# Six instead of four first-product blocks made in halves, with a new order and bank plan, in a linear-attention and FFN kernel

## The chip, the cores and the metric

One core of one Trainium2 chip runs the whole kernel. The metric is the device time of one execution in microseconds (us), lower is better. Engines: TensorE (PE matmuls, PEld weight loads), VectorE (DVE), ScalarE (ACT), GpSimd (POOL) and SyncE (SP), which issues most DMAs here.

## The reference, cut to what matters

```python
def _A_ref(x, wqkv, wo):                      # x: (1, 2048, 512), 32 heads of 16
    qkv = (x @ wqkv).reshape(B, S, 3, H, Dh).transpose(2, 0, 3, 1, 4)
    q, k, v = qkv[0], qkv[1], qkv[2]
    phi = lambda t: jnp.where(t > 0, t + 1, jnp.exp(t)) + 1e-6
    pq, pk = phi(q), phi(k)
    kv = jnp.einsum("bhsd,bhse->bhde", pk, v)
    z = jnp.einsum("bhsd->bhd", pk)
    num = jnp.einsum("bhqd,bhde->bhqe", pq, kv)
    den = jnp.einsum("bhqd,bhd->bhq", pq, z)[..., None] + 1e-6
    return (num / den).transpose(0, 2, 1, 3).reshape(B, S, D) @ wo
def _B_ref(x, w1, w2):                        # w1: (512, 1792), w2: (1792, 512)
    return jnp.maximum(x @ w1, 0) @ w2
h = x + _A_ref(_layernorm(x), wqkv, wo)
out = h + _B_ref(_layernorm(h), w1, w2)
```

All tensors are bf16.

## The kernel before, in words

The 2048 tokens are 16 tiles of 128, in four chunks of 512 (chunk c holds tiles 4c to 4c+3). Nothing is scheduled by a compiler: the string ORDER (L18 to L54) is a list of words, each of them calls one small function with the numbers behind its dots (L563 to L566), and each engine runs its instructions in the order in which the words issued them. Semaphores follow from the data. The last or next to last number of a word on TensorE is mostly the PSUM bank (0 to 7; a bank holds 128 x 512 f32), so the string is also the bank plan. A bank can be written anew only when its last reader has finished.

The words that matter, in the order of a tile's way:

- `lx`, `lk`, `lq`, `lv`, `lo`, `l1`, `l2`: loads of x and of the weights, issued on SP (L220, L226).
- `S.t`, `A.t` (VectorE, L254, L255): statistics and their aggregate of tile t; `R` (ScalarE, L260, L261): 1/sqrt; `N.t` (VectorE, L268): the first layernorm. `T.t.b` (TensorE, L293) and `E.t` (ScalarE, L303) transpose tiles 0 to 4 into lnT; `X.t` (SP, L314) does it by a DMA transpose for the others.
- `K.t.b` (L322) and `Q.c.j.b` (L330): the products for k (of a tile) and q (of a chunk, 128 of the 512 columns). `F`, `U` (ScalarE, L340, L343), `M`, `D` (VectorE, L347, L350) make phi of k out of them, `qF`, `qU`, `qM`, `qD` phi of q (pqT).
- `G.t` (L374) sums over the tokens into banks 4 to 7, `z` (L398), `kv` (L420), `m.j.b` (L432) form what all queries share: the matrix of k and v times wo (m_sb), copied out by `mD` (VectorE) and `mA` (ScalarE).
- `d4.c.b` (TensorE, L446; `d4.2.b.2` does chunks 2 and 3 into two banks), `dl4.c`, `dx4.c` (ScalarE, L452, L457): the reciprocal of the denominator of chunk c. `wb.c` (SP, L474) writes it to DRAM, eight `rb.c.h` (SP, L477; for chunk 0 also `ab` on ScalarE's queue) read it back spread over the partitions, and two `dm.c` (VectorE, L493) multiply pqT by it.
- `h.t.b` (TensorE, L502) gives the attention output of tile t, `hD.t` (VectorE, L508) adds x. `s.t`, `a.t`, `n.t` (VectorE, L256, L257, L276; `nA.t` for tiles 0 and 1 on ScalarE, L282) make the second layernorm without its scale, `x.t` (SP, L315) transposes it by DMA into lnT.
- `p.c.f.b` (L517): block f (of 14) of the FFN's first product for chunk c, four matmuls of 512 tokens. `ph.c.f.b.half` (L526): the same block for 256 of the 512 tokens (half 0: tiles 4c and 4c+1, half 1: 4c+2 and 4c+3), four matmuls of half the width into one half of the bank. `pD.c.f.2` (VectorE, L537) or `pA.c.f.2` (ScalarE, L532) empties two banks, f and f+1, with the relu.
- `f.t.b.f0.n` (L546): the second product of tile t, n of the 14 parts; `fo.t` (VectorE, L554) scales by `r` and adds h, `fd.t` (SP, L561) stores it.

Before the change, after the last Q block TensorE makes four first-half blocks of chunk 0 (f = 2, 3, 0, 1), and then turns to the second halves and whole blocks, which need tiles 2 and 3. The blocks ahead of the first of these hide what tiles 2 and 3 still have to go through: hD, s, a, n and the transposes x.3 and x.2.

Of the kernel before, what the change touches and what calls it, by code (L numbers as in the profile page):

```python
# [16 lines left out]

ORDER = """  # L18
table const lx.0.1 warm.66.7.64 lx.1.1 masks lx.2.1 lk.0.4 lx.3.1 S.0 lx.4.2 S.1 lx.6.2 lq.0.4 A.0 A.1 S.2 R.0.1
warm.2.7 lx.8.4 R.1.1 N.0 lx.12.4 A.2 N.1 T.0.1 R.2.1 T.1.5 E.0 N.2 E.1 T.2.2 S.3 K.0.0 E.2 A.3 S.4 K.2.2.2.2  # L20
R.3.1 K.2.2.0.2 F.0.1 N.3 S.5 U.0.1 T.3.3 K.1.6.0.2 E.3 A.4 A.5 K.1.6.2.2 S.7 R.4.2 K.3.1.0.2 M.0.1 F.1.1 S.6
K.3.1.2.2 U.1.1 Q.0.1.5 N.4 F.2.1 A.6 N.5 A.7 F.3.1 T.4.6 M.1.1 X.5 D.0.1 Q.0.0.4 R.6.2 D.1.1 M.2.1 U.3.1 M.3.1
Q.0.2.0 N.7 lo.0.2 E.4 S.9 X.7 U.2.1 Q.0.3.1 N.6 qU.0.0.2 D.3.1 K.4.2 S.15 X.6 qF.0.0.2 S.8 K.5.3 D.2.1 qM.0.0.2
qF.0.2.2 G.3 A.8 A.9 S.12 R.8.2 G.0 S.14 F.4.2 N.9 G.2 A.12 N.8 X.9 U.4.2 S.13 G.1 A.15 A.14 A.13 qD.0.0.2 X.8
R.12.2 K.6.2 qU.0.2.2 M.4.2 S.11 K.7.3 lv.0.2 R.14.2 N.12 N.13 X.12 K.9.1 S.10 F.6.2 D.4.2 K.8.0 U.6.2 lv.2.2 A.10
M.6.2 X.13 G.4 N.14 U.8.2 N.15 D.6.2 G.5 X.15 F.8.2 za.4.1 G.6 A.11 X.14 M.8.2 K.12.0 R.10.2 qM.0.2.2 N.10 K.13.1
N.11 X.10 D.8.2 G.7 za.6.0 F.12.2 X.11 K.14.2 U.12.2 qD.0.2.2 K.15.3 M.12.2 l1.2.2 za.8.0 l2.0.7 K.10.0 F.14.2
D.12.2 K.11.1 U.14.2 zf G.9 M.14.2 F.10.2 D.14.2 G.8 U.10.2 zhi M.10.2 G.12 zlo D.10.2 G.14 z.1.0 z.2.0 z.3.0
z.0.0 G.15 zc zh d4.0.3 G.11 dl4.0 dx4.0 G.10 wb.0 G.13 lo.2.2 Q.1.0.1 gA.2.2 gD.0.2 rb.0.6 Q.1.1.2 ab.0.3 rb.0.2
ab.0.7 rb.0.4 kv.0.0 kv.2.0 ab.0.1 rb.0.0 kv.1.0 kv.3.0 ab.0.5 l1.0.2 Q.1.3.6 kx qF.1.0.2 Q.1.2.5 qU.1.0.2  # L30
qM.1.0.2 m.0.3 m.1.4 Q.2.3.7 qF.1.2.2 mD.0.2 Q.2.1.1 qU.1.2.2 qM.1.2.2 dm.0.0.2 m.2.3 m.3.4 Q.2.0.0 dm.0.2.2
mA.2.2 qD.1.0.2 h.1.6 qU.2.0.2 qD.1.2.2 h.0.2 hD.1 qF.2.0.2 h.3.3 s.1 hD.0 Q.2.2.6 a.1 s.0 nA.1 d4.1.2 a.0 h.2.1
hD.3 x.1 nA.0 s.3 qF.2.2.2 Q.3.0.5 x.0 a.3 hD.2 dl4.1 Q.3.3.4 n.3 qU.2.2.2 s.2 x.3 Q.3.2.3 a.2 dx4.1 n.2 Q.3.1.6
qM.2.0.2 qF.3.2.2 x.2 qM.2.2.2 ph.0.2.0.0 qU.3.2.2 qM.3.2.2 ph.0.3.1.0 wb.1 ph.0.0.2.0 qF.3.0.2 qD.3.2.2
ph.0.1.3.0 qD.2.2.2 ph.0.1.3.1 qU.3.0.2 ph.0.0.2.1 qM.3.0.2 rb.1.6 p.0.11.7 rb.1.3 pD.0.0.2 rb.1.1 ph.0.3.1.1
rb.1.0 p.0.10.6 qD.2.0.2 rb.1.7 qD.3.0.2 rb.1.4 p.0.9.2 rb.1.2 pD.0.10.2 rb.1.5 p.0.6.5 l2.7.7 d4.2.6.2 ph.0.2.0.1
dl4.2 p.0.5.4 r.0.4 dm.1.0.2 dl4.3 p.0.4.3 dx4.2 dm.1.2.2 h.4.7 pD.0.2.2 wb.2 pA.0.4.2 p.0.7.6 dx4.3 hD.4 p.0.8.1
pD.0.6.2 h.5.7 pD.0.8.2 rb.2.4 p.0.13.4 rb.2.7 rb.2.3 hD.5 h.6.5 rb.2.0 rb.2.6 f.1.2.0.7 hD.6 rb.2.5 s.5 rb.2.2
rb.2.1 p.0.12.3 wb.3 h.7.1 pD.0.12.2 f.0.7.7.7 hD.7 s.4 f.2.4.0.7 s.7 a.5 a.4 dm.2.0.2 f.1.2.7.7 n.4 dm.2.2.2 a.7
n.5 rb.3.2 s.6 rb.3.6 h.9.0 rb.3.3 h.8.1 x.4 hD.9 a.6 f.0.7.0.7 n.7 r.4.4 fo.1 x.7 n.6 s.9 f.3.5.0.7 rb.3.1 x.6  # L40
h.10.0 x.5 h.11.3 f.3.5.7.7 f.2.4.7.7 fo.3 hD.8 fd.3 rb.3.7 p.1.13.2 fo.2 rb.3.4 fd.1 hD.11 p.1.12.1 rb.3.5 a.9
fo.0 fd.2 p.1.2.6 rb.3.0 hD.10 p.1.3.7 pD.1.12.2 p.1.6.0 pD.1.2.2 p.1.0.3 dm.3.0.2 p.1.7.1 dm.3.2.2 h.13.7
pD.1.6.2 p.1.1.4 hD.13 p.1.4.5 pD.1.0.2 p.1.5.6 s.13 p.1.9.3 pD.1.4.2 h.12.7 p.1.8.2 hD.12 s.10 p.1.11.5 s.8
p.1.10.4 pD.1.8.2 h.14.1 s.11 h.15.7 hD.14 a.10 f.7.0.0.7 a.11 n.9 hD.15 n.11 pD.1.10.2 f.6.7.0.7 a.8 n.10 r.8.4
s.14 x.10 f.4.1.0.7 n.8 x.8 f.5.5.0.7 x.9 f.5.5.7.7 x.11 f.4.1.7.7 fo.5 fd.0 s.12 a.13 f.7.0.7.7 a.12 fo.4 a.14
f.6.7.7.7 fo.7 n.14 n.12 s.15 p.2.10.5 fo.6 p.2.11.6 n.13 fd.6 a.15 n.15 r.12.4 x.12 p.2.13.1 p.2.12.0 fd.5 x.13
p.2.9.4 pD.2.12.2 p.2.8.3 x.15 p.2.2.1 pD.2.8.2 x.14 p.2.3.2 pD.2.10.2 p.2.0.3 fd.7 pD.2.2.2 p.2.1.4 p.2.7.6
pD.2.0.2 p.2.6.5 p.3.8.1 pD.2.6.2 p.3.9.2 p.3.12.3 pD.3.8.2 p.3.13.4 p.3.2.0 pD.3.12.2 p.2.4.6 p.3.10.5 p.3.6.1
p.2.5.7 p.3.4.3 pD.2.4.2 p.3.5.4 p.3.7.2 f.11.7.0.7 pD.3.6.2 pD.3.4.2 f.11.7.7.7 p.3.3.1 f.10.3.7.7 pD.3.2.2
p.3.11.6 p.3.0.4 pD.3.10.2 f.8.1.0.7 f.10.3.0.7 p.3.1.5 f.8.1.7.7 pD.3.0.2 fo.10 f.15.0.0.14.3.1 f.15.6.0.14.0.2  # L50
fo.15.3.1 fd.15.3.1 f.13.4.0.7 fo.15.0.2 fd.15.0.2 fd.4 f.13.4.7.7 f.14.5.7.7 fo.13 fo.11 fd.13 fd.10 f.12.6.0.7
fo.8 fd.8 fd.11 f.14.5.0.7 f.9.7.0.7 f.9.7.7.7 f.12.6.7.7 fo.9 fo.14 fd.9 f.15.3.0.14.2.1 fd.14 fo.12 fd.12
fo.15.2.1 fd.15.2.1
"""  # L54


# [540 lines left out]
```

## Time and profile before

| what | us |
|---|---|
| median of 3 runs | 169.82 (169.5 to 170.22) |
| the profiled execution | 169.75 |
| span from its first to its last instruction | 168.0 |
| TensorE busy in the span | 161.2 (96%), granted clock 0.999 |
| VectorE busy | 114.3 (68%) |
| ScalarE busy | 49.4 (29%) |

The profiled execution's own time is 1.75 us longer than its span. In the order of time, a row has its start, its length, the engine, the line of the kernel, the operation and the tiles written and read; consecutive rows of one kind are merged. Matmuls overlap: the next one starts before the end of the one ahead, so a stretch of them is counted from start to start.

### The profile page before, as it was taken

To read this page: it belongs to the slowest core of one execution; us is meant where nothing else is said; L and a number is where in the kernel's file an instruction comes from. 1 tells how busy PE (TensorE), PEld (TensorE's weight loads), DVE (VectorE), ACT (ScalarE), POOL (GpSimd) and SP (SyncE) were. 2 spreads that over 40 slices of the span, in tenths; PEclk is the share of its full clock that TensorE was granted. 3 is DMA by queue.
4 is the path that set the end of the run, shared out by engine and by line. 5 is a ranking of instruction groups with operands and counts; after the bars stand their busy time and mean duration, and the time that the engine had idled before them with its cause. 6 is when DMAs were issued, how large, how long until landed. Compare 5 with 4: busy or idle time off the path is not lost.

```text
span 168.0 us, 2376 instructions
## 1 busy us (share of the span) xinstructions
PE 161.2 (96%) x896; PEld 78.3 (47%) x912; DVE 114.3 (68%) x215; ACT 49.4 (29%) x83; POOL 4.8 (3%) x21
## 2 busy tenths in 40 slices
...
GB/s 112 328 313 156 58 182 105 234 238 96 205 138 35 119 92 248 98 105 7 109 71 153 5 4 0 31 102 23 125 94 4 0 0 0 0 0 59 125 0 101
DMA packets 26091, 16.28 MB, mean 97 GB/s; under 512 B 16096, under 2 KB 25056, under 8 KB 26080
## 3 DMA queue, kind: packets, MB, share of 16 engines
...
q8 instruction: 7, 0.11, 0.3%
...
HBM read 9.96 MB, written 2.62 MB: 75 GB/s over the span
## 4 chain that ended last, share of the span: by engine, by line
PE 84%; DVE 6%; DMA 4%; issue 1%; ACT 1%; SPq 1%; DVEq 0%
PE bk L546 29%; PE bk L517 27%; PE bk L374 8%; PE bk L322 7%; PE bk L502 6%; PE bk L330 4%; DMA x_nat<-in_A_x_dram 2%; DVE h_nat L508 2%; DMA lnT<-hn 1%; PE bk L526 1%; DVE st L256 1%; DVE st L254 1%; SPq L220 1%; DVE pqT L350 1%; PE bk L398 1%
## 5 line engine op out<-in xcount | busy, mean ns | idle before, releaser
L546 PE MATMUL bk<-w_sb,at 128*128 128x512 bf16 (+2 forms) x245 | 49.4, 355 | 0.4
L517 PE MATMUL bk<-lnT,w_sb 128*128 128x512 bf16 x205 | 46.7, 379 | 0.1
L537 DVE TENSOR_SCALAR at<-bk 128x1024 bf16<-128x1024 f32 x27 | 32.5, 1219 | 16.2 <-PE bk L517 15.0
L546 PEld LDWEIGHTS <-at 128*128 128x128 bf16 x252 | 23.5, 98 | 25.2 <-DVE at L537 0.3
L517 PEld LDWEIGHTS <-w_sb 128*128 128x128 bf16 x208 | 20.4, 98 | 23.9
L554 DVE SCALAR_TENSOR_TENSOR gT<-bk,rstd,h_nat 128x512 bf16<-128x512 f32 (+2 forms) x18 | 12.1, 685 | 19.3 <-PE bk L546 13.9
L260 ACT ACTIVATE rstd<-mv,eps 128x2 f32<-128x2 f32 (+2 forms) x14 | 4.1, 293 | 51.7 <-DVE mv L257 48.9
L340 ACT ACTIVATE eb<-bk 128x1024 bf16<-128x1024 f32 (+1 forms) x18 | 16.6, 931 | 4.4 <-PE bk L322 2.6
L343 ACT ACTIVATE rb<-bk 128x1024 bf16<-128x1024 f32 (+1 forms) x18 | 16.5, 930 | 0.0
L502 PE MATMUL bk<-m_sb,pqs 128*128 128x512 bf16 x64 | 15.6, 379 | 0.0
L330 PE MATMUL bk<-lnT,wq_sb 128*128 128x512 bf16 x61 | 15.0, 379 | 0.2
L322 PE MATMUL bk<-wk_sb,lnT 128*128 128x512 bf16 x64 | 14.8, 379 | 0.0
L374 PE MATMUL bk<-at,h_nat 128*128 128x512 bf16 x54 | 13.0, 379 | 0.1
L508 DVE TENSOR_TENSOR h_nat<-bk,x_nat 128x512 bf16<-128x512 f32 x16 | 10.9, 681 | 1.7 <-PE bk L502 1.7
L254 DVE BATCH_NORM_STATS2 st<-x_nat 128x6 f32<-128x512 bf16 x16 | 10.6, 677 | 2.0 <-DMA x_nat<-in_A_x_dram 2.0
L256 DVE BATCH_NORM_STATS2 st<-h_nat 128x6 f32<-128x512 bf16 x16 | 10.8, 685 | 0.1
L502 PEld LDWEIGHTS <-pqs 128*128 128x128 bf16 x64 | 6.2, 98 | 7.6 <-DVE pqs L493 0.5
L374 PEld LDWEIGHTS <-h_nat 128*128 128x128 bf16 x64 | 6.1, 98 | 7.3 <-issue 0.2
L330 PEld LDWEIGHTS <-wq_sb 128*128 128x128 bf16 x64 | 6.2, 98 | 7.1
L322 PEld LDWEIGHTS <-lnT 128*128 128x128 bf16 x64 | 5.9, 98 | 7.5 <-DMA lnT<-h_nat 0.7
L347 DVE TENSOR_SCALAR eb<-eb 128x1024 bf16<-128x1024 bf16 (+1 forms) x18 | 6.7, 386 | 0.7 <-ACT eb L340 0.7
L493 DVE TENSOR_TENSOR pqs<-pqT,rr 128x1024 bf16<-128x1024 bf16 x8 | 5.2, 680 | 1.9 <-DMA rr<-scr 1.9
...
## 6 DMA issues: line engine op xcount, KB each, us to landing
...
out_dram<-gT SPq DMA_DIRECT2D x15, 128.0 KB, 1.9
rr<-scr SPq DMA_DIRECT2D x28, 64.0 KB, 2.6
...
x_nat<-in_A_x_dram SPq DMA_DIRECT2D x4, 128.0 KB, 2.2
...
```

Source lines behind the costliest of these rows:

```text
L254: op_S = lambda t: nc.vector.bn_stats(out=st[:, t, :], in_=x_nat[:, t, :])
L256: op_s = lambda t: nc.vector.bn_stats(out=st2[:, t, :], in_=h_nat[:, t, :])
L322: nc.tensor.matmul(bk[:, b, :], lhsT=lnT[c][:, kd, j * P : (j + 1) * P], rhs=wk_sb[:, kd, :], **part(("k", t), KD),)
L330: nc.tensor.matmul(bk[:, b, :], lhsT=wq_sb[:, kd, j * P : (j + 1) * P], rhs=lnT[c][:, kd, :], start=(kd == 0), stop=(kd == KD - 1),)
L340: nc.scalar.activation(out=buf(eb, kind, i, n), in_=bank(at_bank[kind, i], n), func=ACT.Exp)
L343: nc.scalar.activation(out=buf(rb, kind, i, n), in_=bank(at_bank[kind, i], n), func=ACT.Relu)
L374: nc.tensor.matmul(bk[:, KD + kd, :], lhsT=ln_nat[:, t, kd * P : (kd + 1) * P], rhs=pk(t)[:, 0, :], start=(not stated), stop=(len(stated) ...
L502: nc.tensor.matmul(bk[:, b, :], lhsT=pqs[:, (c * KD + jb) % NQ, j * P : (j + 1) * P], rhs=m_sb[:, jb, :], start=(jb == 0), stop=(jb == KD ...
L508: nc.vector.tensor_tensor(out=h_nat[:, t : t + n, :], in0=bank(at_bank["h", t], n), in1=x_nat[:, t : t + n, :], op=ALU.add,)
L517: nc.tensor.matmul(bk[:, b, :], lhsT=w1_sb[:, kd, f * P : (f + 1) * P], rhs=lnT[c][:, kd, :], start=(kd == 0), stop=(kd == KD - 1),)
L537: nc.vector.tensor_scalar(out=acts[c % 2][:, f : f + n, :], in0=bank(at_bank["p", c, f], n), scalar1=-1.0, scalar2=0.0, op0=ALU.mult, op1= ...
L546: nc.tensor.matmul(bk[:, b, 0 : w * P], lhsT=acts[c % 2][:, f, j * P : (j + 1) * P], rhs=w2_sb[:, f, k * P : (k + w) * P], **part(("f", t, ...
```

## The change

Only ORDER differs. Blocks f = 10 and 11 of chunk 0, which were whole (`p.0.10.6`, `p.0.11.7`), are now made in halves as well, so that six first-half blocks stand ahead of the first second half (`ph.0.10.0.1`). Around it most words stand at other places and in other banks. The lines of the old and the new string at that place:

```diff
-qM.2.0.2 qF.3.2.2 x.2 qM.2.2.2 ph.0.2.0.0 qU.3.2.2 qM.3.2.2 ph.0.3.1.0 wb.1 ph.0.0.2.0 qF.3.0.2 qD.3.2.2
-ph.0.1.3.0 qD.2.2.2 ph.0.1.3.1 qU.3.0.2 ph.0.0.2.1 qM.3.0.2 rb.1.6 p.0.11.7 rb.1.3 pD.0.0.2 rb.1.1 ph.0.3.1.1
...
+n.2 qF.3.2.2 qM.2.0.2 x.2 qM.2.2.2 ph.0.3.3.0 qU.3.2.2 qD.2.2.2 ph.0.0.6.0 ph.0.1.7.0 qM.3.2.2 rb.1.7 qU.3.0.2
+ph.0.2.2.0 qD.3.2.2 rb.1.3 ph.0.11.1.0 rb.1.5 qD.2.0.2 ph.0.10.0.0 qF.3.0.2 rb.1.6 ph.0.10.0.1 rb.1.1 ph.0.11.1.1
```

TensorE's new order from there to the second chunk is: ph.0.3, 0.0, 0.1, 0.2, 0.11, 0.10 (first halves), 0.10, 0.11 (second halves), p.0.5.4, ph.0.2, 0.3, 0.0 (second halves), p.0.6.0, ph.0.1 (second half), p.0.4.3, p.0.7.1, d4.2.5.2, p.0.8.2, p.0.9.3, p.0.13.5, h.4.7, h.6.0, f.3.1.0.7, p.0.12.4, h.7.2, f.3.1.7.7, h.5.4, f.2.3.7.7, f.1.6.0.7, h.8.0, f.1.6.7.7, f.2.3.0.7.

On SP, between the last spread of chunk 0 and the transposes of chunk 1's FFN input (lnT0 is chunk 0, scr1 and rr the denominator of chunk 1), there stood before:

```order
L477 DMA rr_113<-scr0_114 16x4x512 x4
L226 DMA w1_sb_75<-in_B_w1_dram 128x2x1792
L315 DMA_TRANSPOSE lnT0_85<-hn_119 128x4x128 x4
L474 DMA scr1_115<-rd_112 128x512
L477 DMA rr_113<-scr1_115 16x4x512 x8
L226 DMA w2_sb_76<-in_B_w2_dram 128x7x512
```

and there stands now:

```order
L477 DMA rr_113<-scr0_114 16x4x512 x4
L226 DMA w2_sb_76<-in_B_w2_dram 128x7x512
L315 DMA_TRANSPOSE lnT0_85<-hn_119 128x4x128 x2
L474 DMA scr1_115<-rd_112 128x512
L315 DMA_TRANSPOSE lnT0_85<-hn_119 128x4x128 x2
L477 DMA rr_113<-scr1_115 16x4x512 x8
```

The write wb.1 has moved from behind the four transposes x.1, x.0, x.3, x.2 to between x.0 and x.3. The last spreads, rb.3, stand later on SP all eight ahead of chunk 1's four transposes, where these were mixed with them before.

On ScalarE, the two nA and what follows them (L452 is dl4.1, L457 dx4.1), before:

```order
L282 ACTIVATE hn<-h_nat,mv_107 128x512 x2
L340 ACTIVATE eb<-bk 128x1024
L452 ACTIVATE ld<-bk,eps_78 128x512
L343 ACTIVATE rb<-bk 128x1024
L457 ACTIVATE rd<-ld 128x512
L340 ACTIVATE eb<-bk 128x1024
```

and now:

```order
L282 ACTIVATE hn<-h_nat,mv_107 128x512
L452 ACTIVATE ld<-bk,eps_78 128x512
L282 ACTIVATE hn<-h_nat,mv_107 128x512
L457 ACTIVATE rd<-ld 128x512
L340 ACTIVATE eb<-bk 128x1024
L343 ACTIVATE rb<-bk 128x1024
```

dl4.1 stands between nA.1 and nA.0 and dx4.1 right behind nA.0, both ahead of qF.2.2 (L340).

On VectorE, in the second chunk, from the eviction pD.1.8.2 on (at_101 holds the FFN's hidden tokens of chunks 1 and 3), there stands now:

```order
L537 TENSOR_SCALAR at_101<-bk 128x1024
L257 BN_AGGR mv_107<-st_106 128x2
L276 TENSOR_SCALAR hn<-h_nat,mv_107 128x512 x3
L257 BN_AGGR mv_107<-st_106 128x2 x2
L276 TENSOR_SCALAR hn<-h_nat,mv_107 128x512
L508 TENSOR_TENSOR h_nat<-bk,x_nat 128x512
L537 TENSOR_SCALAR at_101<-bk 128x1024
L276 TENSOR_SCALAR hn<-h_nat,mv_107 128x512
```

where, from the second chunk's first eviction pD.1.12.2 on, there stood before:

```order
L537 TENSOR_SCALAR at_101<-bk 128x1024 x2
L493 TENSOR_TENSOR pqs<-pqT_92,rr 128x1024 x2
L537 TENSOR_SCALAR at_101<-bk 128x1024
L508 TENSOR_TENSOR h_nat<-bk,x_nat 128x512
L537 TENSOR_SCALAR at_101<-bk 128x1024
L256 BN_STATS st_106<-h_nat 128x6
```

The products h.8 to h.15 now come ahead of nearly all of the second chunk's first product (dm.3, L493, moved from behind two of its evictions to ahead of all), so n.11, n.13, n.9, n.14 and hD.12 (L508) stand between its first two evictions. TensorE's order there is h.15.2, h.14.7, f.0.0.0.7, p.1.3.5, p.1.8.2, p.1.2.4, h.12.1, p.1.9.3, p.1.7.7, p.1.6.6, p.1.12.0, p.1.11.3, p.1.13.1, p.1.10.2, p.1.0.5, p.1.5.4, p.1.1.6, f.5.2.7.7, p.1.4.3, p.2.2.5, f.5.2.0.7.

Further moves: the four m products go to banks 4, 6, 5 and 7 in a row (before 3, 4 and again 3, 4, with two Q blocks between); T.4 stands behind two Q blocks of chunk 0 instead of one; a.1 stands right behind s.1 on VectorE, where hD.0 was between; of the weights, `l1.0.2` is loaded with `l1.2.2`, `l2.7.7` in the old place of `l1.0.2`, and `l2.0.7` in that of `l2.7.7`; h, f and p of the later chunks are mixed in another way. The count of each engine's instructions is the same but for TensorE's, where two whole blocks of four matmuls became four half blocks of four.

More of the change, by code (lines that the diff above doesn't have):

```diff
@@ L19 @@
 table const lx.0.1 warm.66.7.64 lx.1.1 masks lx.2.1 lk.0.4 lx.3.1 S.0 lx.4.2 S.1 lx.6.2 lq.0.4 A.0 A.1 S.2 R.0.1
[L20 to L33, printed above, removed]
@@ L34 @@
-qM.2.0.2 qF.3.2.2 x.2 qM.2.2.2 ph.0.2.0.0 qU.3.2.2 qM.3.2.2 ph.0.3.1.0 wb.1 ph.0.0.2.0 qF.3.0.2 qD.3.2.2
-ph.0.1.3.0 qD.2.2.2 ph.0.1.3.1 qU.3.0.2 ph.0.0.2.1 qM.3.0.2 rb.1.6 p.0.11.7 rb.1.3 pD.0.0.2 rb.1.1 ph.0.3.1.1
-rb.1.0 p.0.10.6 qD.2.0.2 rb.1.7 qD.3.0.2 rb.1.4 p.0.9.2 rb.1.2 pD.0.10.2 rb.1.5 p.0.6.5 l2.7.7 d4.2.6.2 ph.0.2.0.1
-dl4.2 p.0.5.4 r.0.4 dm.1.0.2 dl4.3 p.0.4.3 dx4.2 dm.1.2.2 h.4.7 pD.0.2.2 wb.2 pA.0.4.2 p.0.7.6 dx4.3 hD.4 p.0.8.1
-pD.0.6.2 h.5.7 pD.0.8.2 rb.2.4 p.0.13.4 rb.2.7 rb.2.3 hD.5 h.6.5 rb.2.0 rb.2.6 f.1.2.0.7 hD.6 rb.2.5 s.5 rb.2.2
@@ L39 @@
[L39 to L53, printed above, removed]
+warm.2.7 lx.8.4 R.1.1 N.0 lx.12.4 A.2 N.1 T.0.1 R.2.1 T.1.6 E.0 N.2 E.1 T.2.4 S.3 K.0.2 E.2 A.3 S.4 K.1.4.2.2
@@ new lines @@
+R.3.1 K.1.4.0.2 F.0.1 N.3 A.4 U.0.1 S.5 T.3.5 K.2.6.2.2 E.3 S.7 K.2.6.0.2 F.1.1 K.3.3.0.2 M.0.1 A.5 U.1.1 D.0.1
+K.3.3.2.2 M.1.1 R.4.2 Q.0.3.1 S.6 F.3.1 A.7 A.6 N.5 F.2.1 Q.0.1.5 N.4 X.5 R.6.2 D.1.1 T.4.7 U.3.1 M.2.1 Q.0.0.4
+M.3.1 S.8 E.4 lo.0.2 U.2.1 S.10 Q.0.2.0 qF.0.0.2 N.6 K.4.2 N.7 X.6 A.10 A.8 qU.0.0.2 S.9 K.5.3 D.3.1 X.7 A.9 D.2.1
+R.8.2 G.0 S.15 F.4.2 N.8 G.1 S.13 X.8 U.4.2 S.14 G.3 qU.0.2.2 A.13 S.12 lv.0.2 G.2 M.4.2 A.12 N.9 K.7.3 R.12.2
+A.15 D.4.2 X.9 qF.0.2.2 K.6.2 N.12 A.14 S.11 R.14.2 X.12 K.8.0 F.6.2 N.15 N.14 G.4 A.11 N.13 U.6.2 M.6.2 X.13
```

26 lines of the change are left out of this document (added).

## Prediction

> **What bounds the kernel now.** I read the busy times by stage first, then who TensorE waited for, then its order of time around the longest wait. The page's head and the stretches (length, then busy time and count of PE, PEld, DVE, ACT, POOL, granted clock, DMA share):
>
> ```profile
> span 168.0 us, 2376 instructions
> ```
> ```profile
> 10.40:54.90 44.50, 44.21 (x256) 20.79 (x260) 36.76 (x84) 32.98 (x49) 0.00 (x0) 1.00 0.54 148
> 54.90:60.00 5.10, 4.50 (x33) 3.03 (x32) 3.55 (x9) 4.29 (x6) 0.00 (x0) 1.00 0.44 97
> 60.00:80.00 20.00, 19.80 (x101) 9.16 (x102) 15.97 (x25) 3.71 (x7) 0.00 (x0) 1.00 0.36 116
> 80.00:105.00 25.00, 24.88 (x114) 11.35 (x116) 19.55 (x32) 0.50 (x2) 0.00 (x0) 1.00 0.22 56
> ```
>
> TensorE is the bound, at full clock: in these 94.6 us it is idle for 1.21 (0.29, 0.60, 0.20 and 0.12), and half of that lies in the 5 us around 57, while VectorE has a fifth of its time free. No matmul is removed, so the change can win only what TensorE waits for, and lose only by new waits. The longest of TensorE's waits behind the first 9 us (in which K.1 and K.2 change places and little else), its rows there, and the chain of waits:
>
> ```profile
> PE bk L526 <- DMA lnT<-hn: 0.6, 1, 0.6
> ```
> ```profile
> 56.09 1.92 PE L526 MATMUL bk<-lnT,w_sb 128*128 128x256 bf16 x16
> 58.62 1.03 PE L526 MATMUL bk<-lnT,w_sb 128*128 128x256 bf16 x8 [0.60 <-DMA lnT<-hn]
> 59.49 1.03 PE L517 MATMUL bk<-lnT,w_sb 128*128 128x512 bf16 x4
> ```
> ```profile
> 56.14 2.43 DMA lnT<-hn
> ...
> 59.65 0.86 PE bk L517 x4
> 60.51 0.44 PE bk L526 x4
> ```
>
> This is the wait that the change speaks to. Matmuls overlap, so I count starts: eight half-width ones from 58.62 to 59.49 are 0.109 us apart. The 17th was thus due at 56.09 + 16 x 0.109 = 57.83 and started at 58.62: **0.79 us lost**, waiting for the landing of x.2 (the transpose of token tile 2). A smaller loss stands at d4.2 (L446); the block ahead of it, and the eviction pD.0.10.2:
>
> ```profile
> 62.30 1.03 PE L517 MATMUL bk<-lnT,w_sb 128*128 128x512 bf16 x4
> 63.47 0.61 PE L446 MATMUL bk<-pqT,zhd 128*32 128x512 bf16 x8
> ```
> ```profile
> 62.03 1.22 DVE L537 TENSOR_SCALAR at<-bk 128x1024 bf16<-128x1024 f32 x1
> ```
>
> Four matmuls of 0.216 (0.86 / 4) from 62.30 reach to 63.16, d4.2 starts at 63.47: **0.31 lost**, waiting for pD.0.10.2, which empties banks 6 and 7 until 63.25.
>
> **More halves.** Twelve half blocks instead of eight are two more whole blocks (0.86) made as four halves (0.44): 4 x 0.44 - 2 x 0.86 = **+0.04 us**. The Trainium skill, page "TensorE: Matmul & The Clock Gate", section "Back-to-back issue gap", speaks against halves: it lets both the weight load and the matmul set the spacing, with 81 ns at 128 columns and 131 ns at 512. A line between these gives an estimate of 98 ns at 256, so by that page two more split blocks would cost 8 x (2 x 98 - 131) ns = 0.5 us, and the time below would be 169.6. The rows here, 0.109 and 0.216 from start to start, differ from both its spacing and its surcharge, and the sum goes by them.
>
> **The wait for x.2.** Six first halves now stand ahead of the first second half: 24 x 0.109 = 2.62 us of cover instead of 1.74, if x.2 doesn't land later. Its way: VectorE's statistics, ScalarE's nA, the transposes on SP.
>
> ```profile
> 49.63 0.69 DVE L256 BATCH_NORM_STATS2 st<-h_nat 128x6 f32<-128x512 bf16 x1
> 50.24 0.67 DVE L508 TENSOR_TENSOR h_nat<-bk,x_nat 128x512 bf16<-128x512 f32 x1
> 50.83 0.17 DVE L257 BATCH_NORM_AGGREGATE mv<-st 128x2 f32<-128x6 f32 x1
> ```
> ```profile
> 51.04 1.58 ACT L282 ACTIVATE hn<-h_nat,mv 128x512 bf16<-128x512 bf16 x2 [1.00 <-DVE mv L257]
> ...
> 53.42 0.68 ACT L452 ACTIVATE ld<-bk,eps 128x512 f32<-128x512 f32 x1
> ```
> ```profile
> 51.78 5.57 SPq L315 DMA_TRANSPOSE lnT<-hn  x4
> 57.45 0.53 SPq L474 DMA_DIRECT2D scr<-rd  x1
> ```
>
> a.1 (50.83) now stands right behind s.1, which ends at 50.32: it runs at 50.36, nA.1 at 50.57, and x.1 is issued at about 51.3 instead of 51.78. hD.0 and all behind it on VectorE come 0.2 later, so nA.0 runs at 52.1 instead of 51.9; dl4.1 (0.68) fits into the gap before it, and dx4.1, about as long, ends behind nA.0 at 53.5. On SP, x.1 and x.0 take until 54.2 (before 54.7), wb.1 now costs 0.5 there, and x.3 and x.2 (1.2 each) start at 54.8 and 56.1, as before (the fourth of 5.57 us began at 56.14). Behind wb.1 wait x.3, x.2 and the eight rb.1, which come no later than before. Landing 2.4 us after issue: 58.5. Six halves starting at 56.05 (0.04 ahead of 56.09, as x.0 lands 0.5 earlier) reach to 58.67. The wait goes; I keep **+0.05** for the rounding: **-0.79 + 0.05**. Late next would be bank 1, which ph.0.11.1.0 takes 0.1 us after qU.3.2.2 frees it. The new thing is a write (wb.1) between transposes. A store between transposes is on SP later on:
>
> ```profile
> 119.23 0.58 SPq L561 DMA_DIRECT2D out_dram<-gT  x1
> 119.90 3.81 SPq L315 DMA_TRANSPOSE lnT<-hn  x3
> ```
>
> Below: nothing, since SP went on there 0.67 behind a store of the same size. Above: the next transposes start only when the write has landed (2.1 us, row below), 1.5 us lost. I take the near end.
>
> **d4.2** takes banks 5 and 6 instead of 6 and 7. From 56.05, twelve halves (12 x 0.436), the wait of 0.05 and four whole blocks (4 x 0.8625) stand ahead of it: 64.8. Bank 6 is emptied by pD.0.0.2. VectorE comes to it behind pD.0.2.2, which waits for ph.0.3.3.1 (nine halves and one block: matmuls to 61.3, release 61.5), and one add of 0.60: 61.5 + 1.13 + 0.60 = 63.2, and its 1.21 end at 64.4. So the 0.31 shrink to a start gap that I leave at 0.1: **-0.2**. If VectorE came 0.5 later there, the 0.31 would be back.
>
> **VectorE's margins.** In the new order its evictions end close before TensorE wants the bank. Steps from one start to the next:
>
> ```profile
> 96.02 0.68 DVE L508 TENSOR_TENSOR h_nat<-bk,x_nat 128x512 bf16<-128x512 f32 x1
> 96.62 1.21 DVE L537 TENSOR_SCALAR at<-bk 128x1024 bf16<-128x1024 f32 x1
> 97.75 0.68 DVE L256 BATCH_NORM_STATS2 st<-h_nat 128x6 f32<-128x512 bf16 x1
> ```
> ```profile
> 106.56 0.17 DVE L257 BATCH_NORM_AGGREGATE mv<-st 128x2 f32<-128x6 f32 x1
> 106.65 0.32 DVE L276 TENSOR_SCALAR hn<-h_nat,mv 128x512 bf16<-128x512 bf16 x1
> 106.89 0.68 DVE L256 BATCH_NORM_STATS2 st<-h_nat 128x6 f32<-128x512 bf16 x1
> ```
>
> and an eviction that waited, with the weight loads of the block that it waited for:
>
> ```profile
> 121.64 3.49 DVE L537 TENSOR_SCALAR at<-bk 128x1024 bf16<-128x1024 f32 x3 [0.50 <-PE bk L517]
> ```
> ```profile
> 120.37 0.75 PEld L517 LDWEIGHTS <-w_sb 128*128 128x128 bf16 x4
> ```
>
> An eviction that waits starts 121.64 - 120.37 = 1.27 after its block's first weight load; it holds VectorE for 1.13, an aggregate for 0.09, an n for 0.24, an add 0.60 (0.68 to its end). The tightest place is p.1.13.1: it needs bank 1, which hD.12 empties. From the weight load of p.1.9.3: 1.27 + pD 1.13 + three aggregates 0.27 + four n 0.96 + hD 0.68 = 4.31, plus 0.05 for the release = 4.36, against five blocks of 0.8625 = 4.31: **+0.05**. The same count gives margins of 0.0 to 0.1 at f.5.2.7.7 (its sixth matmul needs pD.1.12.2), f.5.2.0.7, p.2.4.4 and p.2.13.4; and T.4.7 stands one Q block (0.86) later, while its N.4 gets D.0.1, M.1.1, two aggregates and N.5 ahead of it, about as much. From below each of the five costs nothing (an earlier bank gains nothing on a busy TensorE), from above one more n (0.24): 0 to 1.2. Most steps are rows, so I stay near the lower end, **+0.25** in all.
>
> **Hidden moves.** The four m products go to four banks and no longer wait behind mD; two Q blocks (1.7 us) stand in their place either way. Weights are issued in another order, l2.0.7 last at about 61 with 5 us to land, and its first reader, f.3.1.0.7, starts at 69.9 (counted below). Without that cover TensorE would wait one to one from there on. The last products, fo and fd end in the same steps as before, so the tail stays.
>
> The sum: -0.79 + 0.05 - 0.2 + 0.04 + 0.05 + 0.25 = -0.6. The profiled execution took 169.75 us (1.75 around its span), so **169.1 us**; the median shown, 169.82, is 0.07 above it.
>
> **Rivals.** A measurement of this kernel tells 0.5% from no change, so the bounds are 168.97 and 170.67.
>
> *All margins hold.* Then the +0.25 and half of the rest vanish: 168.8. For it: every term is a row. Against: five places with under 0.1.
>
> *The write holds back the transposes.* x.3 starts 2.1 us after wb.1, x.2 lands 1.5 later, and TensorE waits 1.5 instead of 0.79: 169.75 + 0.7 - 0.2 + 0.3 = 170.5. The Trainium skill, "DMA: Bandwidth & Descriptors", section "Rules for kernel authors", says that a transpose next to ordinary DMAs needs nothing; the trace agrees with the 0.67 at 119.23. A smaller delay, 0.8, would leave 169.8.
>
> *Slower: the spreads of the third and fourth chunk come late.* Rows of the DMA issues, SP and VectorE:
>
> ```profile
> rr<-scr SPq DMA_DIRECT2D x28, 64.0 KB, 2.6
> ...
> scr<-rd SPq DMA_DIRECT2D x4, 128.0 KB, 2.1
> ```
> ```profile
> 66.15 0.34 SPq L474 DMA_DIRECT2D scr<-rd  x1
> 68.56 3.88 SPq L477 DMA_DIRECT2D rr<-scr  x8
> ```
> ```profile
> 65.18 1.29 DVE L493 TENSOR_TENSOR pqs<-pqT,rr 128x1024 bf16<-128x1024 bf16 x2 [1.93 <-DMA rr<-scr]
> ```
>
> d4.2 now starts at 64.9 instead of 63.47, so wb.2 goes out at 67.1 (66.15 - 63.47 = 2.7 later, less 0.5 for r.0.4, which no longer stands between). Its eight spreads are issued from 69.5 (2.41 behind it, as in the rows) to 73.4 and land by 76.0. Their readers, the two dm.2, are wanted by h.8.0, which TensorE reaches at 78.4: 64.9, d4.2 0.7, five whole blocks to f.3.1.0.7 at 69.9, then four f of seven matmuls (1.51 each) and three blocks. Two dm take 0.60 + 0.66, so the spreads may land as late as 77.1: a margin of 1.1. rb.3 follows behind dm.2, now all eight in one go (77.9 to 81.8, landed 84.4), where dm.3 is wanted at about 84.1; behind it stand two dm, six hD, six statistics, four aggregates, two n and a fo, some 10.4 us to 94.5, and pD.1.8.2 waits for p.1.9.3 until 95.2: 0.7 us of slack. VectorE is busy for 19.55 of the 25 us there; once it is later than that slack, every bank of the second chunk comes late, one to one. Spreads that land 2.8 us later than their 2.6 cost 2.8 - 1.1 = 1.7 at h.8.0 and give 170.8. For it: VectorE already lost 1.93 to such spreads. Against: they need twice their time.
>
> **Chances.** The forecast 0.55 (a third of it under 168.97), all margins hold 0.17, the write 0.13, the spreads 0.15. Faster: 0.17 + 0.18 = 0.35; slower 0.15 and 0.02 of the write: 0.17; the same 0.48. Range 168.6 to 170.7: it takes in the first three cases and leaves out the spreads, and a few hundredths below.
>
> **What would show it.** Right: no wait of L526 for the transposes, d4.2 without a gap, under 0.1 us before L517 from 93 to 118. Wrong: L526 waits again and x.2 lands after 59; gaps of TensorE before L517 ended by L508 or L537 around 98 to 118; L293 waiting for L268 at 12; VectorE waiting over 1 us for rr near 76 or 84.

## The result, and the profile after

The changed kernel takes **169.25 us** (median of 8 runs, 168.84 to 169.72) against 170.0 (median of 8, 169.5 to 170.74): a ratio of 0.9945, 95% interval 0.9923 to 0.9966. The prediction was 169.1, with 168.6 to 170.7 as its range. Ratios here and below are worked out from fast executions alone; the only slow ones were two of e7's twelve, at 247.39 and 442.57 us. The profiled execution took 169.35 us. Its page begins:

```profile
span 167.6 us, 2414 instructions
...
PE 162.9 (97%) x920; PEld 79.8 (48%) x920; DVE 115.9 (69%) x215; ACT 49.5 (30%) x83; POOL 4.8 (3%) x21
```

The stretches that the prediction used (length, then busy time and count of PE, PEld, DVE, ACT, POOL, granted clock, DMA share), and after them the whole list of TensorE's waits:

```profile
10.40:54.90 44.50, 44.50 (x262) 20.80 (x260) 37.05 (x85) 33.20 (x50) 0.00 (x0) 1.00 0.53 148
54.90:60.00 5.10, 5.10 (x41) 3.87 (x40) 4.12 (x9) 4.77 (x6) 0.00 (x0) 1.00 0.47 109
60.00:80.00 20.00, 20.00 (x108) 9.58 (x106) 16.19 (x23) 3.72 (x7) 0.00 (x0) 1.00 0.37 114
80.00:105.00 25.00, 25.00 (x117) 11.29 (x116) 24.37 (x48) 0.90 (x4) 0.00 (x0) 1.00 0.33 73
```
```profile
PE bk L251 <- DVE m_sb L192: 1.0, 1, 1.0
PE bk L293 <- DVE h_nat L268: 0.4, 1, 0.4
```

By these rows TensorE is not idle for a moment between 10.4 and 105 us, although VectorE is busy for 24.37 of the 25 us behind 80 (19.55 before). The wait for the transposes is gone; the two waits that are left lie in the first 9 us. TensorE's and SP's order of time at the place of the change:

```profile
56.46 3.66 PE L526 MATMUL bk<-lnT,w_sb 128*128 128x256 bf16 x32
59.95 1.03 PE L517 MATMUL bk<-lnT,w_sb 128*128 128x512 bf16 x4
...
63.43 1.89 PE L517 MATMUL bk<-lnT,w_sb 128*128 128x512 bf16 x8
65.25 0.61 PE L446 MATMUL bk<-pqT,zhd 128*32 128x512 bf16 x8
```
```profile
51.74 2.71 SPq L315 DMA_TRANSPOSE lnT<-hn  x2
54.54 0.53 SPq L474 DMA_DIRECT2D scr<-rd  x1
55.16 2.51 SPq L315 DMA_TRANSPOSE lnT<-hn  x2
```

Start to start, the 32 half-width matmuls (six first and two second halves) take 59.95 - 56.46 = 3.49 us, and 32 x 0.109 = 3.49: nothing is lost at x.2. The same count, start to start less so many matmuls by 0.109 (half width) or 0.2156 (full), is used for every gap below.

The two spans (168.0 and 167.6) show less than half of the gain, since the first Q block of this execution came 0.46 later. From the first weight load of the first Q block to the first of the last product's (x4 of a whole block, x8, and x14 of the last product) the weight loads of before and of after show:

```profile
10.45 0.75 PEld L330 LDWEIGHTS <-wq_sb 128*128 128x128 bf16 x4
...
163.68 0.98 PEld L546 LDWEIGHTS <-at 128*128 128x128 bf16 x14
```
```profile
10.91 1.61 PEld L330 LDWEIGHTS <-wq_sb 128*128 128x128 bf16 x8
...
163.30 0.98 PEld L546 LDWEIGHTS <-at 128*128 128x128 bf16 x14
```

That is 153.23 us before and 152.38 after (from 10.915 to 163.298): **0.85 less**. This stretch is called "the body" below. Each kernel has one profile, so how well the body repeats can only be judged from the four kernels that lose next to nothing in it (after, e5, e9 and e10, 152.27 to 152.40); the start differs by up to 0.84. So each experiment is read by its body beside its time. The tail behind it is 4.32 to 4.35 us in every profile.

### The profile page after: what moved, and what is told of

The parts are those of the page before. It is cut to its first block, busy times and chain, and to the rows that moved or that the text cites. A ratio compares the mean times of both kernels' runs of the same rounds, so it can differ in the third digit from the quotient of the medians.

```text
span 167.6 us, 2414 instructions
## 1 busy us (share of the span) xinstructions
PE 162.9 (97%) x920; PEld 79.8 (48%) x920; DVE 115.9 (69%) x215; ACT 49.5 (30%) x83; POOL 4.8 (3%) x21
## 4 chain that ended last, share of the span: by engine, by line
PE 93%; DVE 2%; DMA 1%; ACT 1%; issue 0%
PE bk L546 28%; PE bk L517 26%; PE bk L374 8%; PE bk L322 8%; PE bk L330 8%; PE bk L502 8%; PE bk L526 3%; DMA x_nat<-in_A_x_dram 1%; DVE st L254 1%; PE bk L446 1%; DVE gT L554 1%; PE bk L398 1%; DVE h_nat L268 1%; PE bk L420 1%; PE bk L432 1%; PE bk L293 1%
## 5 line engine op out<-in xcount | busy, mean ns | idle before, releaser
L546 PE MATMUL bk<-w_sb,at 128*128 128x512 bf16 (+2 forms) x252 | 50.9, 355 | 0.0
L517 PE MATMUL bk<-lnT,w_sb 128*128 128x512 bf16 x200 | 45.6, 379 | 0.0
L517 PEld LDWEIGHTS <-w_sb 128*128 128x128 bf16 x200 | 19.5, 98 | 23.1 <-issue 0.4
L340 ACT ACTIVATE eb<-bk 128x1024 bf16<-128x1024 f32 (+1 forms) x18 | 16.6, 930 | 3.5 <-PE bk L420 1.6
L322 PE MATMUL bk<-wk_sb,lnT 128*128 128x512 bf16 x64 | 15.0, 379 | 0.0
L508 DVE TENSOR_TENSOR h_nat<-bk,x_nat 128x512 bf16<-128x512 f32 x16 | 10.7, 679 | 1.1 <-PE bk L502 1.0
L322 PEld LDWEIGHTS <-lnT 128*128 128x128 bf16 x64 | 6.0, 98 | 7.4 <-DMA lnT<-h_nat 0.4
L268 DVE TENSOR_SCALAR h_nat<-x_nat,mv,rstd 128x512 bf16<-128x512 bf16 x16 | 6.2, 406 | 0.6 <-ACT rstd L261 0.5
```

The source lines that it names most:

```text
L322: nc.tensor.matmul(bk[:, b, :], lhsT=lnT[c][:, kd, j * P : (j + 1) * P], rhs=wk_sb[:, kd, :], **part(("k", t), KD),)
L340: nc.scalar.activation(out=buf(eb, kind, i, n), in_=bank(at_bank[kind, i], n), func=ACT.Exp)
L517: nc.tensor.matmul(bk[:, b, :], lhsT=w1_sb[:, kd, f * P : (f + 1) * P], rhs=lnT[c][:, kd, :], start=(kd == 0), stop=(kd == KD - 1),)
L546: nc.tensor.matmul(bk[:, b, 0 : w * P], lhsT=acts[c % 2][:, f, j * P : (j + 1) * P], rhs=w2_sb[:, f, k * P : (k + w) * P], **part(("f", t, ...
```

## The experiments

Ten kernels were run. In four of them (e1, e2, e7, e10) ORDER takes one line less, and all line numbers behind it are one lower: L525 is ph, L516 p, L445 d4. Ratios are to the kernel before, measured beside them, and need not be the quotient of two medians; single executions of before ranged from 169.49 to 170.75.

**How many halves: four and five in the new order.** Four (e1_new_four):

```diff
-ph.0.11.1.0 rb.1.5 qD.2.0.2 ph.0.10.0.0 qF.3.0.2 rb.1.6 ph.0.10.0.1 rb.1.1 ph.0.11.1.1
+rb.1.5 qD.2.0.2 qF.3.0.2 rb.1.6 p.0.10.0 rb.1.1 p.0.11.1
```

> The new order with blocks 10 and 11 whole again, so that only four first halves stand ahead of the first second half; all else stays. Theory (the gain is the cover for x.2): x.2 lands as in the new kernel, 58.9, and TensorE comes to the second half 8 x 0.109 = 0.87 us earlier, so L526 or L517 waits 0.8 us for the transpose again and the time goes back up by about 0.75, to within 0.2% of the kernel before. Rival (the gain comes from the order around it: banks, d4.2, the start): no such wait, the ratio to the kernel before stays at 0.9945.

Measured: 169.64 us, ratio 0.9985 (0.9965 to 1.0004), body 153.20. The wait is back:

```profile
56.67 1.91 PE L525 MATMUL bk<-lnT,w_sb 128*128 128x256 bf16 x16
59.22 2.75 PE L516 MATMUL bk<-lnT,w_sb 128*128 128x512 bf16 x12 [0.65 <-DMA lnT<-hn]
```

59.22 - 56.67 - 16 x 0.109 = 0.81 us. (The bracket says 0.65, because it counts from the modelled end of the last matmul.) Nothing but two split blocks was taken from after, and the body is that of before again. Five (e2_new_five):

```diff
-ph.0.11.1.0 rb.1.5 qD.2.0.2 ph.0.10.0.0 qF.3.0.2 rb.1.6 ph.0.10.0.1 rb.1.1 ph.0.11.1.1
+ph.0.11.1.0 rb.1.5 qD.2.0.2 qF.3.0.2 rb.1.6 rb.1.1 ph.0.11.1.1 p.0.10.0
```

> The new order with block 10 whole again: five first halves. Theory: each half is 0.44 us of cover, so TensorE waits 0.35 to 0.4 us for x.2, half of the gain is left, ratio to the kernel before 0.997. Rival (a fixed loss that is there or not, like a bank): either 0.9945 as with six or 1.000 as with four.

```profile
55.79 3.07 PE L525 MATMUL bk<-lnT,w_sb 128*128 128x256 bf16 x24
58.70 1.89 PE L516 MATMUL bk<-lnT,w_sb 128*128 128x512 bf16 x8
```

58.70 - 55.79 - 24 x 0.109 = 0.29 us lost, too short for the list of waits; body 152.66, 0.28 above after. The time, 169.0 and ratio 0.9937 (0.9914 to 0.996), does not tell five from six. The loss is a little under the 0.35 to 0.4 expected. So a split block is worth its cover of 0.44, or what is left of the wait if that is less: 0.29 from five to six. (From four to five it is 0.52, of which 0.09 is not cover: in e1 TensorE starts 0.14 behind the landing of x.2, in e2 0.05.)

**The same halves in the old order.** Five (e3_old_five) and six (e4_old_six):

```diff
-ph.0.1.3.0 qD.2.2.2
+ph.0.1.3.0 ph.0.11.7.0 qD.2.2.2
...
-p.0.11.7
+ph.0.11.7.1
```

> The kernel before with block 11 made in halves: five first halves in the old order and banks. Theory: the wait for x.2 falls from 0.77 to 0.33 us, gain 0.4 us, ratio 0.9975. Rival (halves bring nothing without the new order): 1.000, with the wait moved to a bank.

```profile
56.93 2.34 PE L526 MATMUL bk<-lnT,w_sb 128*128 128x256 bf16 x20 [0.30 <-DMA lnT<-hn]
59.44 1.91 PE L526 MATMUL bk<-lnT,w_sb 128*128 128x256 bf16 x16 [0.17 <-DMA lnT<-hn]
...
64.13 0.61 PE L446 MATMUL bk<-pqT,zhd 128*32 128x512 bf16 x8 [0.19 <-DVE at L537]
```

Measured: 170.39 us, ratio 1.0004 (0.9981 to 1.0028), body 153.50. The wait for x.2 shrank to 59.44 - 56.93 - 20 x 0.109 = 0.33, but d4.2 now waits for VectorE, and starts 64.13 - 61.19 - 12 x 0.2156 = 0.35 behind its turn (one of the twelve has no record; 0.09 of it is found in every profile, see below). The first half block waited for x.0 as well, the transpose of tile 0. That belongs to the old order: in all four of its profiles this block's first matmul starts 0.14 us behind the landing of x.0, and TensorE loses 0.05 (before), 0.25 (e3), 0.01 (e4) and 0.14 us (e7) there, start to start, of which the list of waits names only the 0.25. In the new order x.0 lands 0.79 or 0.80 ahead of that matmul.

```diff
-ph.0.1.3.0 qD.2.2.2
+ph.0.1.3.0 ph.0.11.7.0 ph.0.10.6.0 qD.2.2.2
...
-p.0.11.7
+ph.0.11.7.1
...
-p.0.10.6
+ph.0.10.6.1
```

> The kernel before with blocks 10 and 11 made in halves, in their old banks 6 and 7. Bank 6 holds a Q block until qU.3.0.2 ends at 59.19. Theory (the new banks are what makes the sixth half possible): ph.0.10.6.0 would start at 58.27 and waits for ScalarE until 59.25, about 1 us lost instead of 0.77, ratio 1.001. Rival (the count of halves alone does it): no wait, ratio 0.995.

Measured: 170.09 us, ratio 1.0003 (0.9983 to 1.0024), body 153.21. TensorE and VectorE there:

```profile
56.61 5.05 PE L526 MATMUL bk<-lnT,w_sb 128*128 128x256 bf16 x44
61.67 1.89 PE L517 MATMUL bk<-lnT,w_sb 128*128 128x512 bf16 x7
64.00 0.61 PE L446 MATMUL bk<-pqT,zhd 128*32 128x512 bf16 x8 [0.45 <-DVE at L537]
```
```profile
62.73 1.22 DVE L537 TENSOR_SCALAR at<-bk 128x1024 bf16<-128x1024 f32 x1
```

No wait for x.2 is left, and yet nothing is won: d4.2 starts 64.00 - 61.67 - 8 x 0.2156 = 0.61 behind its turn (one of the eight matmuls has no record), since pD.0.10.2, the row of VectorE, empties its banks until 63.95; another 0.26 (61.67 - 56.61 - 44 x 0.109) goes between 56.61 and 61.67, 0.17 of it ahead of p.0.9.2 at 61.67, whose bank 2 pD.0.0.2 empties until 61.62. Together 0.87, about as much as the wait that was removed.

The wait that was expected, for qU.3.0.2 to free bank 6, did not come, and the reason lies in the edit. In this string ph.0.10.6.0 stands ahead of qU.3.0.2, which still has to read the Q block in bank 6. Semaphores follow the order of the words, so the half block overwrites half of that Q block and qU waits for the half block instead of the other way round:

```profile
59.52 1.02 ACT L343 ACTIVATE rb<-bk 128x1024 bf16<-128x1024 f32 x1 [0.68 <-PE bk L526]
```

So e4 computes something else than the other kernels, and no version with six halves in the old banks and all reads in place was run. It shows only that the next banks take the cover back even where bank 6 is not waited for. With e3, whose string has no such fault, the halves alone won nothing that could be measured; that the gain needs the other banks and orders around them rests on the two waits of e4 and on after, which has neither; no run changed the banks alone. In after, d4.2 takes banks 5 and 6, and the eviction of bank 6, pD.0.0.2, ends 0.40 ahead of it:

```profile
63.63 1.22 DVE L537 TENSOR_SCALAR at<-bk 128x1024 bf16<-128x1024 f32 x1
```

**Was d4.2 late before?** The prediction took 0.31 us for it. e7_old_d4_later is the kernel before with d4.2 behind a half block:

```diff
-d4.2.6.2 ph.0.2.0.1 dl4.2
+ph.0.2.0.1 d4.2.6.2 dl4.2
```

> The kernel before with d4.2 made one step later: the half block ph.0.2.0.1 (0.44 us) goes ahead of it instead of behind. The prediction's step: before, TensorE lost 0.31 us ahead of d4.2 because pD.0.10.2 empties banks 6 and 7 until 63.25; then, 0.44 later, d4.2 finds its banks free, the stretch from the first Q block's first weight load to the last product's is 152.92 us instead of 153.23, and the time is 0.3 below before (ratio about 0.998). Rival theory, which the weight loads suggest: before, the fourth matmul of p.0.6.5 was made at about 63.16 and is only missing from the records, so nothing was lost: the stretch stays within 0.08 of 153.23 and the ratio within 0.002 of 1.000.

Measured: 170.13 us, ratio 1.0008 (0.999 to 1.0027), body 153.33. Nothing is won, so before nothing was lost: the body is 0.09 longer (153.325 against 153.233), a hundredth more than the rival allowed, and the longer wait for x.0 (0.14 instead of 0.05) accounts for it. The records of before say why. Its matmuls and its weight loads of the three whole blocks ahead of d4.2 (whose row, at 63.47, stands in the prediction):

```profile
60.79 2.54 PE L517 MATMUL bk<-lnT,w_sb 128*128 128x512 bf16 x11
```
```profile
60.68 2.37 PEld L517 LDWEIGHTS <-w_sb 128*128 128x128 bf16 x12
```

Twelve weight loads, eleven matmuls: the last one, due at 63.16, has no record, and the gap was its place. From 60.79, twelve matmuls reach to 63.38, and d4.2 starts 0.09 behind. In after it is 65.25 - 63.43 - 8 x 0.2156 = 0.09 too.

**Does the write between the transposes hold them back?** e5_write_behind:

```diff
-n.3 wb.1 Q.3.3.1
+n.3 Q.3.3.1
...
-x.2 qM.2.2.2
+x.2 wb.1 qM.2.2.2
```

> The kernel after with the write wb.1 moved from between x.0 and x.3 to behind x.2; all else as after. My reading of the profile after: a write between transposes costs SP its own issue, about 0.5 us, and nothing more. Then x.3 and x.2 go out 0.3 to 0.6 us earlier, each still lands 2.4 us after its issue, TensorE (which waits for none of them in the kernel after) gains nothing, the eight rb.1 go out 1.5 to 2 us later and dm.1 some 0.5 to 1.5 us later, hidden: the time is that of after, a ratio of 0.9945 to before, give or take 0.002. Rival, the write holds back the transposes behind it: x.3 lands over 0.5 us sooner after its own issue than the 2.41 us of after. Second rival, dm.1 is late for h.4: TensorE waits at L517's neighbours around 69 us and the time is above 169.5.

```profile
51.08 5.68 SPq L315 DMA_TRANSPOSE lnT<-hn  x4
56.85 0.53 SPq L474 DMA_DIRECT2D scr<-rd  x1
```

The four transposes take SP from 51.08 to 56.76, 5.68 us, where with the write among them it was 51.74 to 57.67, 5.93: the write of 0.53 costs them 0.25. (The rest falls into a pause that SP has there anyway: without the write, 0.47 lie between x.0 and x.3, against 0.09 between x.3 and x.2.) x.3, right behind the write, lands 2.41 behind its issue with it and 2.40 without it, x.2 2.43 both times (56.45 to 58.88 and 55.54 to 57.97). The time is 169.14, ratio 0.9945 (0.9923 to 0.9966), the body 152.27, 0.11 below after's; 0.07 of that is only this profile's first Q weight load, which comes 0.14 ahead of its matmul instead of 0.21. The write's price is its place on the queue, no more; the spreads, which go out later here, stay hidden.

**Five halves, and the write behind.** e10_five_write_behind joins e2 and e5 (both edits above).

> The kernel after with five split blocks instead of six (block 10 whole, as in e2_new_five) and the write wb.1 behind x.2 (as in e5_write_behind). Theory: cover and landing simply add up. In e2_new_five TensorE lost 0.28 us waiting for x.2, in e5_write_behind x.2 was issued 0.37 earlier, so together nothing is lost at x.2, the stretch from the first Q block's first weight load to the last product's is 152.3 us, as in after (152.38), and the ratio to before 0.9945 give or take 0.002. Rival, the sixth split block is needed for something else (a bank or the next transposes): the stretch is 152.6 or more, with a gap of 0.2 us or more between 57 and 60 us.

```profile
56.48 2.82 PE L525 MATMUL bk<-lnT,w_sb 128*128 128x256 bf16 x24
59.13 1.89 PE L516 MATMUL bk<-lnT,w_sb 128*128 128x512 bf16 x8
```

59.13 - 56.48 - 24 x 0.109 = 0.03; body 152.40; 169.13 us, ratio 0.9952 (0.9929 to 0.9975). Cover and landing add up: 0.29 missing in e2, an earlier landing here, nothing lost. The sixth split block and the write's place are two ways to the same end.

**A tight margin of VectorE.** e6_tight_margin makes VectorE later ahead of p.1.13.1:

```diff
-p.1.11.3 hD.12
+p.1.11.3 n.14 n.14 hD.12
```

> The kernel after with two n.14 more (repeats that write the same values) on VectorE ahead of hD.12. They hold VectorE 0.24 us each, 0.48 in all. Theory, the margin of p.1.13.1 is what the traces of after show, about 0.06 us, and VectorE works without a pause behind it until about 105: TensorE loses about 0.4 us there (0.48 less 0.06), one gap ahead of p.1.13.1 and further ones at the next tight places (f.5.2.7.7, p.2.2.5, p.2.4.4) that add little as VectorE is then late only once; the time is 169.6 to 169.7, 0.4 above after. If the prediction's price of that margin were right (TensorE already loses 0.05 there and 0.25 in all), the loss would be 0.48 and the gap there 0.53. Rival, VectorE has slack there (a pause between its instructions takes the two up): no gap, 169.25.

VectorE at that place in after, then in e6, and TensorE in e6:

```profile
97.35 0.24 DVE L257 BATCH_NORM_AGGREGATE mv<-st 128x2 f32<-128x6 f32 x2
97.56 0.35 DVE L276 TENSOR_SCALAR hn<-h_nat,mv 128x512 bf16<-128x512 bf16 x1
97.83 0.68 DVE L508 TENSOR_TENSOR h_nat<-bk,x_nat 128x512 bf16<-128x512 f32 x1
```
```profile
96.88 0.24 DVE L257 BATCH_NORM_AGGREGATE mv<-st 128x2 f32<-128x6 f32 x2
97.09 1.13 DVE L276 TENSOR_SCALAR hn<-h_nat,mv 128x512 bf16<-128x512 bf16 x3
98.14 0.68 DVE L508 TENSOR_TENSOR h_nat<-bk,x_nat 128x512 bf16<-128x512 f32 x1
```
```profile
94.69 3.62 PE L517 MATMUL bk<-lnT,w_sb 128*128 128x512 bf16 x16
98.87 1.46 PE L517 MATMUL bk<-lnT,w_sb 128*128 128x512 bf16 x6 [0.56 <-DVE h_nat L508]
```

The two repeats held VectorE for (98.14 - 96.88) - (97.83 - 97.35) = 0.78, more than the 0.48 expected (each repeat writes the tile that the one ahead has written, and starts 0.04 behind its end). TensorE lost 98.87 - 94.69 - 16 x 0.2156 = 0.73: one to one, less a margin of **0.05**. No second gap follows. The time is 169.64, ratio 0.9984 (0.9969 to 0.9999), the body 153.07, 0.69 above after's. So the margin is as tight as the prediction counted, and on its other side: it holds.

**The prediction's slower rival, made to happen.** e8_spreads_late delays wb.2 on ScalarE:

```diff
-p.0.9.3 dx4.2 p.0.13.5
+p.0.9.3 dl4.3 dl4.3 dl4.3 dl4.3 dl4.3 dx4.2 p.0.13.5
```

> The kernel after with five dl4.3 more (repeats that write the same values) on ScalarE ahead of dx4.2, so that the write wb.2 and its spreads rb.2 go out about 2.9 us later: wb.2 at about 70.4, the last rb.2 landed at about 78.6 instead of 75.7. Theory of the rival in the prediction: the margin is what the trace of after shows, dm.2 done 0.72 us before h.8.0's first weight load; dm.2 then ends at about 79.9 and TensorE waits about 1.3 us at h.8.0 (L508's producer, the block h.8.0 behind L493), and up to 0.4 us more ahead of pD.1.8.2's bank, as VectorE has 0.46 us of slack there: 170.5 to 171.0. Other theory, the spreads are hidden anyway (their time varies and the readers can wait): 169.25, no wait of TensorE near 78.

SP, VectorE and TensorE of e8, and then the two rows of after that answer to the first and the third:

```profile
70.94 0.34 SPq L474 DMA_DIRECT2D scr<-rd  x1
```
```profile
78.85 1.29 DVE L493 TENSOR_TENSOR pqs<-pqT,rr 128x1024 bf16<-128x1024 bf16 x2 [2.39 <-DMA scr<-rd]
```
```profile
75.56 3.19 PE L546 MATMUL bk<-w_sb,at 128*128 128x512 bf16 x14
80.20 1.04 PE L502 MATMUL bk<-m_sb,pqs 128*128 128x512 bf16 x4 [1.45 <-DVE pqs L493]
```
```profile
67.51 0.34 SPq L474 DMA_DIRECT2D scr<-rd  x1
```
```profile
75.73 3.19 PE L546 MATMUL bk<-w_sb,at 128*128 128x512 bf16 x14
78.75 1.03 PE L502 MATMUL bk<-m_sb,pqs 128*128 128x512 bf16 x4
```

Counted from the first Q block, the write went out 3.58 later (the five repeats), the last of its spreads landed 3.01 later, dm.2 ended 2.47 later (at 80.14 instead of 77.82), and TensorE lost 80.20 - 75.56 - 14 x 0.2156 = 1.62 at h.8.0: 170.8 us, ratio 1.0052 (1.0031 to 1.0074), body 153.99, 1.61 above after's. The margin between dm.2 and h.8.0 is thus 2.47 - 1.62 = 0.85, that of the spreads' landing 3.01 - 1.62 = 1.39; the extra 0.4 thought possible ahead of pD.1.8.2 didn't come. The rival's place was right, and beyond the margin its price, one to one; in the kernel after the spreads are simply on time.

**The start.** e9_warm_through fills TensorE's pause ahead of the first transposes:

```diff
-warm.2.7 lx.8.4
+warm.2.7 warm.12.7.64 lx.8.4
```

> The kernel after with one more group of warm-up matmuls (64 columns, results unused) right behind warm.2.7, which fills TensorE's pause from about 4.7 to 6 us before the first transposes T.0 to T.2. Theory, the transposes that follow a pause start 0.107 us apart instead of 0.054 because the array stood idle, and the first Q block waits on that: with the pause filled T.0 to T.2 start 0.054 apart and the first Q weight load comes up to 0.3 us sooner, 169.0 to 169.25, at most a ratio of 0.993 to before. Rival, the start is set by the landing of the loads and VectorE's statistics: the spacing changes or not, the first Q block comes at the same place behind lx.2's landing, and the time is that of after, 169.25 give or take 0.2. If the warm-up reaches past the landing, T.0 comes later and the time is up to 0.5 above.

The weight loads of the transposes and of the first K block (L322), in after and then in e9:

```profile
6.03 0.77 PEld L293 LDWEIGHTS <-h_nat 128*128 128x128 bf16 x8 [1.33 <-DVE h_nat L268]
7.12 0.23 PEld L293 LDWEIGHTS <-h_nat 128*128 128x128 bf16 x4 [0.32 <-DVE h_nat L268]
7.32 0.35 PEld L322 LDWEIGHTS <-lnT 128*128 128x128 bf16 x3
```
```profile
6.01 1.10 PEld L293 LDWEIGHTS <-h_nat 128*128 128x128 bf16 x12
7.36 0.33 PEld L322 LDWEIGHTS <-lnT 128*128 128x128 bf16 x3 [0.25 <-ACT lnT L303]
```

Most of e9's twelve are still 0.107 apart, with no pause ahead of them, while after's third four, behind a wait of 0.32, come within 0.13 us. So do the first four, behind a pause, in eight of the twelve profiles (before's from 5.41 to 5.53). The theory that an idle array makes the first ones slow falls, and their cause stays open. The K block starts at the same place as in after, whose own start was a late one (last section). 169.22 us, ratio 0.995 (0.9935 to 0.9966), body 152.35: nothing is won. The added group ran until 6.0, past the 5.4 at which T.0 starts in most executions, so what a shorter group would do wasn't tried.

No version here beats the kernel after by more than the measurement can tell. From the first Q block to the last product, no two neighbouring matmuls of after are more than 0.03 us further apart than their widths ask for, but for about 0.1 ahead of and behind each d4.

## Why the prediction came out

The time was right, by a mechanism that was right, two wrong terms of opposite sign, and some luck in the base.

- **The wait for x.2 (-0.79, +0.05):** right. It is gone, and e1 brings back 0.81, e2 0.29. The steps behind it hold too. Counted from each profile's first Q weight load, which is 0.46 later in after, x.1 was issued at 51.28 (said: 51.3), x.2 at 55.99 (56.1) and landed at 58.42 (58.5), the halves started at 56.00 (56.05), d4.2 at 64.78 (64.8). In after the six halves reach to 56.46 + 24 x 0.109 = 59.08 and x.2 lands at 58.88, with 0.2 to spare. The 0.05 kept for rounding was not lost.
- **d4.2 (-0.2):** wrong, and this is the step that failed: "Four matmuls of 0.216 (0.86 / 4) from 62.30 reach to 63.16, d4.2 starts at 63.47: 0.31 lost". The first matmul of that row belonged to the block ahead, and the block's own last one, due at 63.16, has no record. The list of TensorE's waits had no wait of L446, but it could not decide: it leaves out e2's 0.29 too. e7 shows that there was nothing to win. e3 and e4 show the wait that the prediction described, in the kernel where it does occur, and there the list names it.
- **VectorE's margins (+0.25 in five places, +0.05 at p.1.13.1):** the count was nearly right and the price wrong. hD.12 freed its bank with 0.05 to spare, by e6, where the prediction's steps gave 0.05 too late; no matmul lost anything between 80 and 105. The other four places were not tried one by one. A margin of 0.05 costs nothing until it is passed, and then everything beyond it.
- **Halves (+0.04):** no gap is seen for them. The Trainium skill's page "TensorE: Matmul & The Clock Gate", section "Back-to-back issue gap", would have given an estimate of 0.5 us more for two split blocks; after's 32 half-width matmuls start 0.109 apart, half of a whole one's, and the measurement decides against that estimate.
- **The sum:** -0.79 for the wait, and about -0.1 ahead of it (the first halves start 45.54 behind the first Q block instead of 45.64), make the body's -0.85 to within 0.04. Half of that 0.1 is the wait for x.0, which the prediction had seen (0.04); the rest wasn't traced. The prediction's -0.6 holds -0.2 that wasn't there, and 0.35 for rounding, margins and p.1.13.1 that wasn't lost. That the time still came within 0.15 is in part luck: the sum starts from one execution of 169.75, and the eight of before have a median of 170.0. The change itself was -0.75 between the medians and -0.85 in the body, against -0.6. The prediction's rival "all margins hold" took 0.95 off and so 0.1 too much, for the same false 0.2.
- **The write:** e5 shows it cost 0.25 on SP. The Trainium skill, "DMA: Bandwidth & Descriptors", section "Rules for kernel authors", says that a transpose next to ordinary DMAs needs nothing. The sentence is about transposes that corrupt each other and promises nothing on time, so it could not settle this rival; the trace agrees with it, since x.3 went out 1.28 us before the write ahead of it had landed (55.16 and 56.44).
- **The spreads:** on time; by e8 they could have landed 1.39 later, where 1.1 was counted.

Of the idle 1.21 us that opened the prediction, 0.60 is the wait for x.2; most of the rest is missing records. In the stretch up to 54.90 TensorE has 256 matmuls and 0.29 idle before, while e7, whose order is the same up to there, has 262 and none; from 60 to 105 e7 has no idle time either, where before has 0.32.
